# Sliding-window attention with a gated convolution on one Trainium2 core: the band mask of 18 of 32 score units moved from VectorE into TensorE's sum

## Chip, core and metric

The kernel runs on one core of one Trainium2 chip. The metric is the device time of one execution in microseconds, lower is better. Before the change it takes 223.1 us (median of three runs: 222.8, 223.1, 225.12).

The page names the engines PE (TensorE, matmuls), PEld (its weight loads), DVE (VectorE), ACT (ScalarE), POOL (GpSimd) and SP (SyncE, which here only issues DMAs).

## What is computed

Eight batches, eight heads, 576 positions, head size 64. Each position attends to the positions at most 32 away; the result feeds a feed-forward block with a three-tap convolution along the sequence as its gate.

```python
scores = scale * np.matmul(q, k.transpose(0, 1, 3, 2))
mask = np.abs(pos[:, None] - pos[None, :]) <= 32
scores = np.where(mask, scores, -1000000000.0)
attn = softmax(scores)                      # over the last axis
x = (attn @ v), heads side by side          # (8, 576, 512)
h = np.maximum(x @ w_in, 0.0)               # (8, 576, 1024)
conv_out[:, s] = sum over k of conv_w[k] * h[:, s + k - 1]
out = (h * sigmoid(conv_out)) @ w_out       # (8, 576, 512)
```

## The kernel before

**Order.** The whole kernel is one list of steps, the string `ORDER` (lines 29 to 96). Each word is a step with its arguments, and a number behind `@` is the PSUM bank it starts at. The steps are issued in this order, and a pinning helper at line 175 keeps every engine to it, so nearly all instructions carry line 175 in the profile and groups are told apart by their tiles. An engine that waits holds up all that stands behind it in its own queue.

**Attention.** A batch `b` has two groups `G` of four heads. `lq`, `lk`, `lv` load float32 q, k, v through SP's queue; `cq`, `ck`, `cv`, `vo` cast them to bf16 (last argument: `p` POOL, `a` ACT, `d` DVE; `vo` is v shifted by 64 rows); `tq`, `tk` transpose q and k on DVE (tiles `qT`, `kT`). Each group is cut into two halves `h` of four or five blocks of 64 queries, which gives 8 x 2 x 2 = 32 score units. For one unit:

- `sc` (line 240) makes the scores of 64 queries against 128 keys per block and head in four PSUM banks, one bank per head. Each head lies on 32 partitions with two bf16 halves (`e`) of its 64 dimensions, so a block takes 4 heads x 2 = 8 matmuls of 32 rows and 64 columns: 32 (h = 0) or 40 (h = 1) in a unit.
- `ex` takes the exponential on ACT into the tile `attn`, 1024 or 1280 columns.
- `mk` (line 266) multiplies `attn` by a 0/1 band on DVE, in place.
- `av` multiplies with v on PE; a column of ones in v makes the sums. `nr` takes the reciprocal of these and scales on DVE into the tile `xn`.

`xt` transposes `xn` into `xT` by DMA; the first two batches do it on PE (`xp`) with a copy (`xe`).

**Feed-forward.** The sequence is cut into chunks of 384 rows, three for two batches, 12 in all; the first two chunks are worked in halves, which gives 14 pieces `P`. For each piece and each quarter `m2` of the 1024 channels: `ph` (8 matmuls with `w_in`), `re` (ReLU on ACT), `pc` (convolution), `th` (tanh on ACT), `ga` (gate on DVE, into `gT`). The convolution has several forms: `P` six full matmuls; `A` and `D` twelve matmuls of 64 x 64, of which `A` then takes three ACT instructions in `th` and two DVE instructions in `ga`, and `D` one ACT and three DVE instructions; `X` no matmul, but two ACT instructions and four DVE instructions (`tp`). Each chunk ends with three `py` (8 matmuls of 512 columns with `w_out`), `ye` (copy out of PSUM) and `st` (store).

**Start.** `li`, `ci` load and cast `w_in`, `lo`, `co` `w_out`; `cw`, `dg` make diagonal matrices of the convolution weights; `s0` to `s7` fill constants.

Of the kernel before, what the change touches and what calls it, by code (L numbers as in the profile page):

```python
# [34 lines left out]
av,0,0,1@4 lv,1,0 ci,2,p ph,0,0@0 nr,0,0,1 ci,3,p ph,0,2@6 re,0,0 lo,2 pc,0,0,P@7 re,0,2 ci,1,p xp,0,3@4 th,0,0,P
xp,0,4@5 lo,3 xe,0,3,a ph,0,3@6 ga,0,0,P ck,1,0,p xe,0,4,a xp,0,2@4 re,0,3 ph,0,1@7 xe,0,2,a lo,1 cq,1,0,p tk,1,0
pc,0,3,P@5 re,0,1 ph,1,3@4 th,0,3,P tq,1,0 lk,2,1 cq,1,1,p pc,0,1,P@6 re,1,3 ph,2,0@7 th,0,1,P ga,0,3,P sc,1,0,0@0
re,2,0 lo,0 ck,1,1,p tq,1,1 ph,2,2@4 ex,1,0,0 ph,1,0@5 ga,0,1,P re,2,2 lv,1,3 cv,1,1,p sc,1,0,1@0 mk,1,0,0,d re,1,0
ph,2,3@4 ex,1,0,1 tk,1,1 lv,1,4 cv,1,2,p pc,0,2,P@5 ph,2,1@6 re,2,3 vo,1,1,d th,0,2,P lk,2,0 cv,1,0,p sc,1,1,0@0
re,2,1 ph,1,2@4 ga,0,2,P ex,1,1,0 mk,1,0,1,d pc,1,0,P@5 lq,2,0 co,2,p re,1,2 mk,1,1,0,d ph,1,1@6 th,1,0,P pc,1,2,P@4  # L40
vo,1,0,d re,1,1 lq,2,1 co,3,p sc,1,1,1@0 th,1,2,P ga,1,0,P pc,1,3,P@6 ex,1,1,1 ga,1,2,P pc,1,1,P@5 lk,3,0 co,1,p s6
pc,2,1,P@4 th,1,3,P mk,1,1,1,d av,1,1,0@0 th,1,1,P av,1,0,0@2 th,2,1,P lv,2,1 ck,2,1,p ga,1,1,P pc,2,0,P@7 nr,1,0,0
pc,2,3,P@5 th,2,0,P nr,1,1,0 pc,2,2,P@2 lq,3,0 co,0,p tk,2,1 xp,1,1@3 xp,1,0@0 xe,1,1,a py,0,0@1 lv,2,0 cv,1,3,p
xe,1,0,a ga,1,3,P ga,2,0,P th,2,2,P lk,4,0 vo,1,2,d cv,1,4,a py,0,2@0 ye,0,0,a vo,1,3,d th,2,3,P lv,2,2 ck,2,0,p
ga,2,1,P ph,3,2@1 ga,2,3,P ye,0,2,a ga,2,2,P ph,3,0@3 st,0,0 cq,2,0,p re,3,2 tk,2,0 av,1,1,1@4 re,3,0 av,1,0,1@6
nr,1,1,1 lk,3,1 cq,2,1,p py,1,0@0 nr,1,0,1 lq,3,1 ck,3,0,p ph,3,3@4 tq,2,1 ye,1,0,a xp,1,2@1 lv,2,3 cv,2,1,p re,3,3
pc,3,2,P@0 tq,2,0 xe,1,2,a sc,2,1,0@2 th,3,2,P ph,3,1@6 ex,2,1,0 st,1,0 ga,3,2,P cq,3,0,p xp,1,3@1 tk,3,0 pc,3,0,P@7
re,3,1 xe,1,3,a xp,1,4@4 lv,2,4 cv,2,0,p pc,3,3,P@5 th,3,0,P mk,2,1,0,d pc,3,1,P@6 xe,1,4,a vo,2,0,d sc,2,1,1@0 st,0,2
ck,4,0,p th,3,1,P py,0,1@4 ex,2,1,1 ga,3,1,P ga,3,0,P lq,4,0 tq,3,0 th,3,3,P cv,2,2,p lq,4,1 sc,2,0,0@0 ye,0,1,a
ph,4,0@6 vo,2,1,p ga,3,3,P ex,2,0,0 tk,4,0 st,0,1 sc,2,0,1@0 ck,3,1,p re,4,0 ph,4,2@4 mk,2,1,1,d ex,2,0,1 lv,3,1  # L50
mk,2,0,0,d cq,3,1,p pc,4,0,P@6 tk,3,1 re,4,2 lk,4,1 cv,2,3,p av,2,0,0@0 lv,3,0 th,4,0,P mk,2,0,1,d vo,2,2,p av,2,1,0@2
py,1,1@4 ga,4,0,P lk,5,1 cv,2,4,p tq,3,1 lv,3,2 ph,4,3@6 vo,2,3,p ye,1,1,a nr,2,0,0 lq,5,0 pc,4,2,A@4 nr,2,1,0 re,4,3
cq,4,0,p av,2,1,1@0 th,4,2,A lv,3,4 pc,4,3,A@2 nr,2,1,1 cq,4,1,p av,2,0,1@6 xt,2,0 th,4,3,A ga,4,2,A ph,4,1@0 cv,3,1,p
xt,2,1 nr,2,0,1 re,4,1 ga,4,3,A sc,3,0,0@4 ck,4,1,p xt,2,2 pc,4,1,P@0 ex,3,0,0 tq,4,0 cv,3,0,p sc,3,1,0@2 th,4,1,P
lv,3,3 mk,3,0,0,d py,1,2@6 vo,3,0,p ex,3,1,0 ga,4,1,P xt,2,3 mk,3,1,0,d py,2,1@7 ye,1,2,a cv,3,2,p xt,2,4 vo,3,1,d
cq,5,0,p sc,3,0,1@0 ye,2,1,a lk,5,0 av,3,1,0@4 tk,4,1 ex,3,0,1 py,2,2@6 st,1,1 cv,3,4,p nr,3,1,0 lv,4,0 ck,5,1,p
mk,3,0,1,d lv,4,1 av,3,0,0@4 sc,3,1,1@0 st,2,1 nr,3,0,0 py,2,0@7 ex,3,1,1 tq,5,0 xt,3,1 cv,3,3,p tq,4,1 vo,3,2,p
sc,4,0,0@0 ye,2,0,a ph,5,0@4 ex,4,0,0 xt,3,0 vo,3,3,d ph,5,2@0 ck,5,0,p re,5,0 st,1,2 mk,4,0,0,d ye,2,2,a lq,6,0
mk,3,1,1,d ph,5,3@2 lq,5,1 re,5,2 tk,5,0 st,2,2 cv,4,0,p av,3,0,1@0 re,5,3 av,3,1,1@4 nr,3,0,1 lv,4,2 cv,4,1,p
pc,5,2,D@6 st,2,0 vo,4,0,p pc,5,0,A@2 nr,3,1,1 th,5,2,D lv,4,4 ph,5,1@0 th,5,0,A lv,4,3 ga,5,2,D xt,3,3 ph,6,2@4  # L60
re,5,1 ga,5,0,A pc,5,1,X@6 pc,5,3,A@0 cq,6,0,p lk,6,0 re,6,2 tp,5,1,X ph,6,0@2 th,5,3,A xt,3,4 cq,5,1,p ph,6,1@4
re,6,0 ga,5,3,A xt,3,2 th,5,1,X pc,6,2,A@2 cv,4,2,p re,6,1 ga,5,1,X pc,6,0,A@0 th,6,2,A lq,6,1 pc,6,1,A@4 vo,4,1,d
lk,7,0 py,3,1@6 cv,4,4,p lq,7,0 th,6,0,A ga,6,2,A lv,5,1 cv,4,3,p th,6,1,A ga,6,0,A py,3,0@7 lq,7,1 vo,4,3,d ye,3,1,a
vo,4,2,d sc,4,1,1@0 lk,6,1 ck,6,0,p ye,3,0,a py,3,2@6 ex,4,1,1 st,3,1 ga,6,1,A lv,5,2 mk,4,1,1,d sc,4,0,1@0 ye,3,2,a
ph,7,1@4 lv,5,3 tk,5,1 ex,4,0,1 tq,5,1 ph,6,3@6 re,7,1 st,3,0 mk,4,0,1,d cq,6,1,p av,4,0,0@4 re,6,3 lv,5,0 sc,4,1,0@0
nr,4,0,0 ex,4,1,0 pc,6,3,A@6 tk,6,0 lv,5,4 cv,5,1,p ph,7,0@4 th,6,3,A mk,4,1,0,d ck,7,0,p lk,7,1 pc,7,1,A@0 ga,6,3,A
re,7,0 av,4,1,0@2 th,7,1,A pc,7,0,A@4 tq,6,0 st,3,2 ck,6,1,p py,4,0@6 th,7,0,A ga,7,1,A cq,7,0,p nr,4,1,0 av,4,1,1@0
ye,4,0,a cv,5,2,p ga,7,0,A xt,4,0 av,4,0,1@2 py,4,1@6 cv,5,3,p nr,4,1,1 xt,4,1 nr,4,0,1 ph,7,2@0 ye,4,1,a cv,5,0,p
vo,5,1,d xt,4,2 sc,5,1,0@2 re,7,2 cv,5,4,p py,4,2@6 vo,5,0,d ex,5,1,0 xt,4,3 vo,5,3,d sc,5,0,0@0 ye,4,2,a lv,6,1
ph,7,3@4 ex,5,0,0 lv,6,0 mk,5,1,0,d xt,4,4 vo,5,2,d av,5,1,0@6 re,7,3 pc,7,2,A@0 mk,5,0,0,d lv,6,4 ph,8,0@2 th,7,2,A  # L70
nr,5,1,0 lv,6,3 st,4,0 cv,6,1,p lv,6,2 av,5,0,0@4 ga,7,2,A re,8,0 pc,7,3,A@6 st,4,1 st,4,2 nr,5,0,0 pc,8,0,A@2
cv,6,0,p th,7,3,A ph,8,3@0 xt,5,0 vo,6,0,d th,8,0,A ga,7,3,A ph,8,1@4 cv,6,4,p lv,7,0 re,8,3 ga,8,0,A xt,5,1 py,5,0@6
cv,6,3,p re,8,1 vo,6,3,d pc,8,1,X@0 sc,5,1,1@2 lv,7,4 tp,8,1,X ye,5,0,a cv,6,2,p py,5,2@7 ex,5,1,1 st,5,0 vo,6,1,p
pc,8,3,A@2 mk,5,1,1,d th,8,1,X vo,6,2,p lv,7,1 ph,8,2@4 tq,7,0 ye,5,2,a th,8,3,A st,5,2 lv,7,3 ga,8,1,X ph,9,3@6
# [559 lines left out]
```

## Time and profile before

| | |
|---|---|
| median of three runs | 223.1 us |
| the profiled execution | 223.78 us |
| its span on the core | 221.8 us |
| TensorE's granted clock | 1.00 of full speed |
| PE busy | 192.9 us (87%) |
| DVE busy | 190.1 us (86%) |
| ACT busy | 162.3 us (73%) |
| POOL busy | 94.2 us (42%) |

The span counts from the first to the last recorded instruction; about 2 us of the execution lie outside it. Busy time of PE counts pipelined matmuls from start to modelled end, so it contains short gaps between matmuls. A group's mean is the time of one instruction from start to end; where instructions follow each other closely they start somewhat sooner than that.

### The profile page before, as it was taken

To read this page: it belongs to the slowest core of one execution; us is meant where nothing else is said; L and a number is where in the kernel's file an instruction comes from. 1 tells how busy PE (TensorE), PEld (TensorE's weight loads), DVE (VectorE), ACT (ScalarE), POOL (GpSimd) and SP (SyncE) were. 2 spreads that over 40 slices of the span, in tenths; PEclk is the share of its full clock that TensorE was granted. 3 is DMA by queue.
4 is the path that set the end of the run, shared out by engine and by line. 5 is a ranking of instruction groups with operands and counts; after the bars stand their busy time and mean duration, and the time that the engine had idled before them with its cause. 6 is when DMAs were issued, how large, how long until landed. Compare 5 with 4: busy or idle time off the path is not lost.

```text
span 221.8 us, 7235 instructions
## 1 busy us (share of the span) xinstructions
PE 192.9 (87%) x3026; PEld 114.5 (52%) x3026; DVE 190.1 (86%) x321; ACT 162.3 (73%) x260; POOL 94.2 (42%) x113
## 2 busy tenths in 40 slices
PE   1044999799999899899998999999999999999993
...
DVE  4989688999999989999999788996998777999820
...
DMA  6999989999999999999998999814204361121323
GB/s 214 333 263 386 339 254 351 354 318 350 284 313 300 137 133 258 250 260 193 369 332 178 222 230 244 222 53 106 98 3 145 69 136 50 38 79 42 142 101 136
DMA packets 65348, 45.96 MB, mean 207 GB/s; under 512 B 53516, under 2 KB 55588, under 8 KB 65316
## 3 DMA queue, kind: packets, MB, share of 16 engines
...
## 4 chain that ended last, share of the span: by engine, by line
PE 41%; DVE 40%; ACT 9%; issue 4%; POOL 3%; DMA 1%; ACTq 0%; DVEq 0%; POOLq 0%
PE PS L175 41%; DVE gT L175 9%; DVE attn L175 6%; DVE xn L175 6%; DVE kT L175 5%; DVE vo L175 5%; DVE qT L175 4%; ACT hT L175 3%; ACT z L175 3%; DVE diag_w L175 2%; ACT attn L175 2%; POOL qb L175 2%; DVE PS L175 2%; ACT PS L175 2%; DMA conv_w<-in_moe_conv_w_dram 1%
## 5 line engine op out<-in xcount | busy, mean ns | idle before, releaser
L175 PE MATMUL PS<-xT,w_in_sb 128*128 128x385 bf16 (+3 forms) x448 | 71.4, 309 | 1.2 <-DVE xn L175 0.5
L175 PE MATMUL PS<-w_out_sb,gT 128*128 128x512 bf16 x288 | 66.7, 380 | 0.1
L175 PEld LDWEIGHTS <-w_in_sb 128*128 128x128 bf16 x448 | 41.5, 100 | 25.7 <-issue 5.2
L175 POOL TENSOR_SCALAR qb<-st 128x1152 bf16<-128x1152 f32 x31 | 37.6, 1214 | 40.2 <-issue 8.9
L175 ACT ACTIVATE hT<-PS 128x770 bf16<-128x770 f32 (+3 forms) x56 | 40.2, 721 | 11.8 <-PE PS L175 10.8
L175 ACT ACTIVATE attn<-PS 128x1024 bf16<-128x1024 f32 (+1 forms) x32 | 36.0, 1132 | 11.2 <-PE PS L175 11.2
L175 DVE SCALAR_TENSOR_TENSOR gT<-PS,hT 128x384 bf16<-128x384 f32 (+2 forms) x66 | 40.2, 617 | 4.2 <-ACT PS L175 3.4
L175 PEld LDWEIGHTS <-gT 128*128 128x128 bf16 x288 | 26.5, 98 | 30.2 <-issue 0.9
L175 ACT ACTIVATE PS<-PS 128x384 f32<-128x384 f32 (+1 forms) x56 | 31.9, 572 | 6.2 <-PE PS L175 5.0
L175 POOL TENSOR_SCALAR ve<-vst 128x512 bf16<-128x512 f32 x38 | 28.4, 754 | 15.5 <-PE PS L175 11.6
L175 DVE TENSOR_TENSOR attn<-attn,mask 128x1024 bf16<-128x1024 bf16 (+1 forms) x32 | 29.3, 923 | 6.2 <-ACT attn L175 6.0
L175 ACT COPY y<-PS 128x512 f32<-128x512 f32 x36 | 20.8, 585 | 17.7 <-PE PS L175 17.7
L175 PE MATMUL PS<-hT,diag_w 64*64 64x384 bf16 (+2 forms) x456 | 31.1, 311 | 2.8 <-DVE gT L175 1.2
L175 DVE TENSOR_TENSOR xn<-PS,rec 128x512 bf16<-128x512 f32 (+1 forms) x32 | 26.4, 824 | 1.4 <-DVE rec L175 0.3
L175 PE MATMUL PS<-qT,kT 32*128 32x64 bf16 x1152 | 15.4, 195 | 11.7 <-DVE kT L175 9.3
L175 ACT ACTIVATE z<-PS 64x384 f32<-64x384 f32 x48 | 23.3, 485 | 0.9
L175 PEld LDWEIGHTS <-diag_w 64*64 64x64 bf16 (+1 forms) x456 | 18.3, 104 | 10.2 <-issue 6.3
L175 PEld LDWEIGHTS <-kT 32*128 32x128 bf16 x1152 | 11.9, 96 | 20.1 <-DVE kT L175 10.2
L175 DVE SCALAR_TENSOR_TENSOR PS<-hT,conv_w_sb,PS 128x384 f32<-128x384 bf16 x36 | 19.6, 618 | 1.6 <-ACT PS L175 1.6
L175 DVE STREAM_TRANSPOSE kT<-qb 128x576 uint32<-128x576 uint32 x16 | 19.7, 1240 | 0.7 <-PE PS L175 0.7
L175 PE MATMUL PS<-ve,attn 128*64 128x65 bf16 x384 | 16.4, 203 | 3.8 <-DVE attn L175 2.2
L175 DVE STREAM_TRANSPOSE qT<-qb 128x576 uint32<-128x576 uint32 x16 | 19.6, 1244 | 0.0
...
## 6 DMA issues: line engine op xcount, KB each, us to landing
...
```

The source lines that it names most:

```text
L175: return lambda *args, **kwargs: tc.keep_in_program_order(do(*args, **kwargs))
```

## The change

Three things change. First, `sc` gets an argument: in 18 of the 32 units (`m`) two constant matrices, `far` (a band of 0 and -1e9) and `unit` (an identity), are multiplied into the four banks before the scores are added on top: 8 matmuls more per unit, 32 rows each, 256 or 320 columns. These units have no `mk`. The other 14 units (`d`) are as before. Two new start-up steps make the matrices: `s9` on POOL for the first 32 partitions, `s10` copies them on ACT to the other three groups of 32. Second, the very last projection (chunk 11, rows 256 to 383) is made, copied and stored in two halves of 256 columns. Third, the whole of `ORDER` is new, and with it the place of many steps and the engine of some.

```diff
-    def sc(b, G, h, bank):
+    def sc(b, G, h, on, bank):
         where["sc", b, G, h] = bank
         qT, kT = qT_[unit(b, G) % NQT], kT_[unit(b, G) % NQT]
-        t0 = tiles_of(h)[0]
-        for t in tiles_of(h):
+        ts = tiles_of(h)
+        if on == "m":
             for e in range(2):
                 for a in range(4):
                     tensor.matmul(
-                        PS[:, bank + a, 64 * (t - t0):64 * (t - t0) + 64],
+                        PS[:, bank + a, 0:64 * len(ts)], far[32 * a:32 * a + 32, e, :],
+                        unit_[32 * a:32 * a + 32, e, None, :].broadcast_to([32, len(ts), 64]),
+                        start=(e == 0), stop=False,
+                    )
+        for i, t in enumerate(ts):
+            for e in range(2):
+                for a in range(4):
+                    tensor.matmul(
+                        PS[:, bank + a, 64 * i:64 * i + 64],
                         kT[32 * a:32 * a + 32, 64 * t:64 * t + 128, e],
                         qT[32 * a:32 * a + 32, 64 * t:64 * t + 64, e],
-                        start=(e == 0), stop=(e == 1),
+                        start=(e == 0 and on != "m"),
+                        stop=(e == 1 and (on != "m" or t == ts[-1])),
                     )
...
-    def py(c, i, bank):
-        where["py", c, i] = bank
+    def py(c, i, *x_bank):
+        *x, bank = x_bank
+        x = x[0] if x else None
+        where["py", c, i, x] = bank
+        n = d_model if x is None else 256
         for m in range(MB):
             tensor.matmul(
-                PS[:, bank, :], gT_[c % 3][:, m, 128 * i:128 * i + 128], w_out_sb[:, m, :],
+                PS[:, bank, 0:n], gT_[c % 3][:, m, 128 * i:128 * i + 128], w_out_sb[:, m, part(x)],
                 start=(m == 0), stop=(m == MB - 1),
             )
...
+    def s9():
+        gpsimd.memset(far[0:32], 0.0)
+        for base, sign in ((0, -1), (64, 1)):
+            gpsimd.affine_select(
+                out=far[0:32], in_=far[0:32], compare_op=ALU.is_ge, fill=-1e9, base=base,
+                pattern=[[32 * sign, 2], [-sign, 128]], channel_multiplier=sign,
+            )
+        gpsimd.memset(unit_[0:32], 0.0)
+        gpsimd.affine_select(
+            out=unit_[0:32], in_=unit_[0:32], compare_op=ALU.not_equal, fill=1.0, base=0,
+            pattern=[[-32, 2], [1, 64]], channel_multiplier=-1,
+        )
+
+    def s10():
+        for a in range(1, 4):
+            scalar.copy(out=far[32 * a:32 * a + 32], in_=far[0:32])
+            scalar.copy(out=unit_[32 * a:32 * a + 32], in_=unit_[0:32])
```

Of the new `ORDER`, the start and the end:

```diff
-lq,0,1 s3 s1 lq,0,0 s2 cw@0 lv,0,1 s5 s0 s7 lk,0,1 dg,4,d lk,0,0 lv,0,2 dg,2,d lv,0,3 dg,1,d cq,0,1,a lv,0,0 dg,7,d
-lv,0,4 dg,6,d dg,0,d li,0 cq,0,0,p tq,0,1 li,2 cv,0,1,p dg,5,d tq,0,0 li,3 ck,0,1,p s4 tk,0,1 li,1 ck,0,0,p dg,3,d
-sc,0,1,0@0 lk,1,0 cv,0,2,p sc,0,1,1@4 tk,0,0 ex,0,1,0 vo,0,1,p lq,1,0 ex,0,1,1 mk,0,1,0,d sc,0,0,0@0 lq,1,1 ex,0,0,0
+lv,0,2 s4 s1 s5 lq,0,0 s3 s2 lk,0,0 s0 lk,0,1 s7 lq,0,1 s9 lv,0,0 cw@0 lv,0,1 dg,4,d s10 li,2 dg,7,d li,0 dg,2,d
+dg,5,d lv,0,3 cq,0,0,a dg,6,d dg,3,d cv,0,2,a lv,0,4 ck,0,0,p tq,0,0 dg,0,d lq,1,1 ck,0,1,p tk,0,0 dg,1,d li,1
+cq,0,1,p sc,0,0,1,m@0 tk,0,1 sc,0,0,0,m@4 ex,0,0,1 li,3 cv,0,0,p tq,0,1 ex,0,0,0 lk,1,1 cv,0,1,p sc,0,1,0,m@0 vo,0,0,d
+sc,0,1,1,m@4 ex,0,1,0 lq,1,0 ci,2,p vo,0,1,d ex,0,1,1 lv,1,0 ci,0,p av,0,1,0@0 av,0,0,0@2 nr,0,1,0 lv,1,1 cv,0,3,a
+vo,0,2,p nr,0,0,0 lo,0 xp,0,1@0 xp,0,0@1 cv,0,4,p xe,0,1,a xe,0,0,a lk,1,0 cq,1,1,p vo,0,3,d ph,0,0@0 ph,0,2@1 re,0,0
...
-pc,13,1,A@6 ga,13,2,X ye,9,2,a pc,13,3,A@4 st,9,2 th,13,1,A py,10,0@0 th,13,3,A ga,13,1,A py,10,2@1 ye,10,0,a
-ga,13,3,A st,10,0 py,11,0@0 ye,10,2,a st,10,2 py,11,1@1 ye,11,0,a st,11,0 py,11,2@0 ye,11,1,a st,11,1 ye,11,2,a
-st,11,2
+re,13,2 tp,13,0,X py,10,0@0 re,13,3 th,13,1,X pc,13,3,A@2 ye,10,0,a ga,13,1,X th,13,0,X st,10,0 pc,13,2,D@0 py,10,2@4
+ga,13,0,X th,13,2,D ga,13,2,D th,13,3,A py,10,1@5 ye,10,2,a ga,13,3,A st,10,2 py,11,0@4 ye,10,1,a st,10,1 py,11,1@5
+ye,11,0,a st,11,0 py,11,2,0@4 ye,11,1,d py,11,2,1@6 st,11,1 ye,11,2,0,a st,11,2,0 ye,11,2,1,a st,11,2,1
```

Counted over the whole list, the steps whose number changes:

| step | before | after |
|---|---|---|
| `mk`, h = 0 / h = 1 | 16 / 16 | 6 / 8 |
| `sc` with the band, h = 0 / h = 1 | 0 / 0 | 10 / 8 |
| `cv` on POOL / ACT / DVE | 38 / 2 / 0 | 30 / 9 / 1 |
| convolution of a full piece: `P` / `A` / `D` / `X` | 2 / 24 / 5 / 9 | 0 / 18 / 15 / 7 |
| convolution of a half piece: `P` / `X` | 16 / 0 | 15 / 1 |
| `xe` on ACT / DVE | 10 / 0 | 9 / 1 |
| `ye` on ACT / DVE | 36 / 0 | 35 (two of 256 columns) / 2 |

The units with the band by batch 0 to 7: 4, 3, 4, 1, 4, 1, 1, 0.

More of the change, by code (lines that the diff above doesn't have):

```diff
@@ L35 @@
[L35 to L74, printed above, removed]
@@ new lines @@
+lo,2 ci,1,p pc,0,0,P@0 re,0,2 tq,1,1 av,0,0,1@2 th,0,0,P lv,1,4 av,0,1,1@4 ci,3,p ga,0,0,P ph,0,1@1 nr,0,0,1
+pc,0,2,P@0 re,0,1 lo,1 ck,1,1,p ph,0,3@6 nr,0,1,1 th,0,2,P pc,0,1,P@7 re,0,3 ga,0,2,P lo,3 cq,1,0,p xp,0,3@4 th,0,1,P
+pc,0,3,P@5 tk,1,1 xe,0,3,a xp,0,2@6 th,0,3,P xp,0,4@0 lv,1,3 cv,1,0,p xe,0,2,a tq,1,0 xe,0,4,a ph,1,1@4 lv,1,2
+cv,1,1,p ga,0,3,P ph,2,0@6 re,1,1 ga,0,1,P vo,1,0,p ph,1,0@5 re,2,0 lk,3,0 pc,2,0,X@4 pc,1,1,P@7 re,1,0 sc,1,1,0,d@0
+tp,2,0,X co,0,p th,1,1,P ph,1,3@6 ex,1,1,0 lv,2,0 pc,1,0,P@5 ga,1,1,P ck,1,0,p re,1,3 ph,2,2@0 mk,1,1,0,d th,2,0,X
@@ new lines @@
+lk,2,0 co,2,p th,1,0,P pc,1,3,P@6 re,2,2 ph,2,1@7 tk,1,0 lq,2,0 ph,2,3@0 re,2,1 cv,1,4,p ga,2,0,X ph,1,2@7 re,2,3
+ga,1,0,P lk,2,1 co,1,p sc,1,0,0,m@0 re,1,2 th,1,3,P pc,2,3,P@4 ex,1,0,0 ga,1,3,P pc,1,2,P@5 lq,3,0 co,3,p th,2,3,P
+sc,1,0,1,m@0 th,1,2,P s6 ga,2,3,P lq,2,1 cv,1,3,p py,0,0@6 ex,1,0,1 ga,1,2,P vo,1,3,d cv,1,2,a lv,2,4 py,0,1@7
+vo,1,2,d vo,1,1,d lv,2,3 av,1,0,1@4 ye,0,0,d ye,0,1,a lv,2,2 cv,2,0,p av,1,1,0@0 nr,1,0,1 av,1,0,0@2 py,0,2@6 st,0,0
+ck,2,0,p nr,1,1,0 nr,1,0,0 pc,2,1,P@7 lv,2,1 cq,2,0,p ye,0,2,a tk,2,0 xp,1,1@4 th,2,1,P xp,1,0@5 xe,1,1,a sc,1,1,1,m@0
@@ new lines @@
+pc,6,3,A@0 ck,6,1,p re,7,0 av,4,0,1@4 cv,5,1,a av,4,1,0@2 cq,6,1,p nr,4,0,1 th,6,3,A ph,7,1@6 nr,4,1,0 vo,5,0,p
+ph,7,3@4 re,7,1 ga,6,3,A xt,4,1 cv,5,2,p sc,4,1,1,m@0 re,7,3 vo,5,1,p xt,4,0 pc,7,0,A@6 tk,6,0 ex,4,1,1 py,4,1@4
+cv,5,3,p th,7,0,A lv,6,1 tq,6,0 lv,6,0 vo,5,2,p av,4,1,1@0 ga,7,0,A ye,4,1,a pc,7,3,A@2 st,4,1 ck,7,0,p nr,4,1,1
+pc,7,1,D@4 lv,6,2 th,7,3,A py,4,0@6 cq,7,0,p xt,4,4 th,7,1,D ga,7,3,A cv,5,4,p ga,7,1,D sc,5,1,0,m@0 ye,4,0,a xt,4,2
+cv,6,1,p ph,7,2@6 ex,5,1,0 vo,5,3,d xt,4,3 cv,6,0,p sc,5,0,0,d@0 re,7,2 py,4,2@4 vo,6,0,d ex,5,0,0 lv,6,3 lv,6,4
@@ new lines @@
+th,8,2,A ga,8,1,D py,5,0@2 th,8,3,D ga,8,2,A ph,9,0@4 ye,5,0,a ga,8,3,D st,5,0 av,5,1,1@0 re,9,0 pc,9,3,D@2 nr,5,1,1
+cv,7,2,p cv,7,0,a pc,9,0,A@4 cv,7,4,a cv,7,3,p pc,9,1,A@6 cv,7,1,d xt,5,2 th,9,0,A vo,7,3,p py,6,1@0 th,9,1,A ga,9,0,A
+xt,5,4 py,6,2@1 ye,6,1,a vo,7,1,p ga,9,1,A th,9,3,D xt,5,3 ga,9,3,D sc,6,0,1,d@4 vo,7,0,p ye,6,2,a py,6,0@0 st,6,1
+ex,6,0,1 st,6,2 vo,7,2,p mk,6,0,1,d sc,6,0,0,d@2 ye,6,0,a ph,10,3@6 ex,6,0,0 st,6,0 tk,7,1 sc,6,1,1,d@0 re,10,3
+ph,10,1@4 mk,6,0,0,d ex,6,1,1 tq,7,1 av,6,0,1@6 re,10,1 sc,6,1,0,m@0 nr,6,0,1 pc,9,2,A@4 ex,6,1,0 mk,6,1,1,d
@@ new lines @@
+av,6,0,0@6 th,9,2,A av,6,1,0@0 nr,6,0,0 ph,10,0@2 nr,6,1,0 av,6,1,1@6 ga,9,2,A xt,6,1 re,10,0 pc,10,1,A@0 nr,6,1,1
+pc,10,0,D@2 th,10,1,A xt,6,0 pc,10,3,D@4 py,7,1@6 th,10,0,D ga,10,1,A xt,6,2 ga,10,0,D ph,10,2@0 ye,7,1,a xt,6,3
+th,10,3,D py,7,0@2 re,10,2 ga,10,3,D st,7,1 pc,10,2,X@6 xt,6,4 py,7,2@3 ye,7,0,a tp,10,2,X st,7,0 ph,11,0@4 ye,7,2,a
+st,7,2 th,10,2,X ph,11,1@0 re,11,0 ga,10,2,X sc,7,1,0,d@2 re,11,1 py,8,1@6 ex,7,1,0 mk,7,1,0,d sc,7,0,0,d@0 ye,8,1,a
+pc,11,0,D@4 ex,7,0,0 st,8,1 py,8,0@6 th,11,0,D mk,7,0,0,d ga,11,0,D av,7,0,0@0 ye,8,0,a ph,11,2@2 st,8,0 nr,7,0,0
@@ L154 @@
     mask = tiles(1, [128, 4 * 5 * 64], BF16, "mask")[0]
+    far = tiles(1, [128, 2, 128], BF16, "far")[0]
+    unit_ = tiles(1, [128, 2, 64], BF16, "unit")[0]
     mask1 = tiles(1, [128, 64], BF16, "mask1_")[0]
@@ L492, with part, ye, sto @@
     out_rows = out.rearrange("b s f -> (b s) f")
-    def py(c, i, bank):
-        where["py", c, i] = bank
+    def part(x):
+        return slice(0, d_model) if x is None else slice(256 * x, 256 * x + 256)
+    def py(c, i, *x_bank):
[3 more added lines that the diff above has]
+        n = d_model if x is None else 256
         for m in range(MB):
             tensor.matmul(
-                PS[:, bank, :], gT_[c % 3][:, m, 128 * i:128 * i + 128], w_out_sb[:, m, :],
+                PS[:, bank, 0:n], gT_[c % 3][:, m, 128 * i:128 * i + 128], w_out_sb[:, m, part(x)],
                 start=(m == 0), stop=(m == MB - 1),
             )
-    def ye(c, i, e):
-        copy(e, y_[(3 * c + i) % NY], PS[:, where["py", c, i], :])
-    def sto(c, i, e="s"):
+    def ye(c, i, *x_e):
+        *x, e = x_e
+        x = x[0] if x else None
+        n = d_model if x is None else 256
+        copy(e, y_[(3 * c + i) % NY][:, part(x)], PS[:, where["py", c, i, x], 0:n])
+    def sto(c, i, x=None):
         r0 = c * CH + 128 * i
-        {"s": sync, "a": scalar}[e].dma_start(out_rows[r0:r0 + 128, :], y_[(3 * c + i) % NY])
+        sync.dma_start(out_rows[r0:r0 + 128, part(x)], y_[(3 * c + i) % NY][:, part(x)])
     def li(p, e="s"):
```

53 lines of the change are left out of this document (32 added, 21 removed).

## The prediction

> **What bounds the kernel now.** I read the page first. Two engines are nearly full and share the chain that ended last; the slices show DVE full in the first two thirds, PE at the end, and the DMA engines full for the first 26 slices (143 us).
>
> ```profile
> PE 192.9 (87%) x3026; PEld 114.5 (52%) x3026; DVE 190.1 (86%) x321; ACT 162.3 (73%) x260; POOL 94.2 (42%) x113
> ...
> PE   1044999799999899899998999999999999999993
> ...
> DVE  4989688999999989999999788996998777999820
> ...
> DMA  6999989999999999999998999814204361121323
> ...
> PE 41%; DVE 40%; ACT 9%; issue 4%; POOL 3%; DMA 1%; ACTq 0%; DVEq 0%; POOLq 0%
> ```
>
> Next the windows of 10 us (start:end, length, busy and count of PE, PEld, DVE, ACT, POOL, clock, DMA share, GB/s):
>
> ```profile
> 60.00:70.00 10.00, 9.04 (x151) 5.09 (x154) 9.92 (x14) 5.76 (x9) 9.32 (x11) 1.00 1.03 303
> 70.00:80.00 10.00, 8.78 (x165) 4.66 (x155) 9.83 (x17) 7.46 (x12) 8.66 (x10) 1.00 1.36 181
> 160.00:170.00 10.00, 10.00 (x144) 5.18 (x142) 9.81 (x20) 9.39 (x16) 0.00 (x0) 1.00 0.18 49
> 200.00:210.00 10.00, 9.96 (x70) 4.81 (x69) 9.25 (x15) 9.49 (x17) 0.00 (x0) 1.00 0.18 71
> ```
>
> From 40 to 120 us DVE is at 91 to 99% and PE has holes; after 120 PE is full. The chain in order of time agrees: mostly DVE pieces up to 119 us, then long PE pieces such as these (start, length, what):
>
> ```profile
> 119.14 8.72 PE PS L175 x145
> ...
> 152.02 18.22 PE PS L175 x288
> ...
> 200.29 17.82 PE PS L175 x104
> 218.13 0.58 ACT y L175
> ```
>
> Last, prices, from the groups with shapes kept apart (busy time, mean ns) and from the timeline (start, length):
>
> ```profile
> L175 DVE TENSOR_TENSOR attn<-attn,mask 128x1280 bf16<-128x1280 bf16 x16 | 15.4, 964 | 2.1 <-ACT attn L175 2.1
> L175 DVE TENSOR_TENSOR attn<-attn,mask 128x1024 bf16<-128x1024 bf16 x16 | 14.1, 881 | 4.0 <-ACT attn L175 3.9
> ```
>
> ```profile
> 85.57 0.42 PE L175 MATMUL PS<-qT,kT 32*128 32x64 bf16 x32
> 85.92 4.09 PE L175 MATMUL PS<-xT,w_in_sb 128*128 128x385 bf16 x24
> ...
> 208.18 1.17 PE L175 MATMUL PS<-hT,diag_w 64*64 64x384 bf16 x24
> 209.29 8.81 PE L175 MATMUL PS<-w_out_sb,gT 128*128 128x512 bf16 x40
> ```
>
> A unit of 32 score matmuls holds the queue from 85.57 to 85.92, 0.35 us, 11 ns each. Forty matmuls of 512 columns take 8.81 us, some 0.17 of it the drain of the last: 216 ns each, 0.42 ns a column. Twenty-four convolution matmuls of 384 columns take 1.11 us to the next start, 46 ns each, where one alone streams 384 x 0.42 = 161: nearly four run at once.
>
> **The masks.** Removed on DVE: 10 x 0.881 + 8 x 0.964 = 16.5 us. Added on PE: 8 matmuls a unit. No row shows 32 rows with 256 columns. From below: four at once, as the convolution, give two rounds of 256 x 0.42 = 0.21 us, 0.27 for 320 columns. From above: one after the other, 8 x 256 x 0.42 = 0.86, and 1.08. The score matmuls are the nearest row: same 32-row groups, same four banks, and they start every 11 ns although 64 columns stream in 27, so at least 2.4 run at once. I take 0.23 and 0.28: 10 x 0.23 + 8 x 0.28 = 4.5 us (ends 4.3 and 17.2; no gain is possible, since the score matmuls stay). The Trainium skill (TensorE: Matmul & The Clock Gate, Part 3, measured speedup) has four row tiles 3.07 times as fast as one, not 4 times; by that figure the sum would be an estimated 5.6 us, and no row here shows it.
>
> `av` no longer stands behind `mk`. The new matmuls wait only for their banks. `s9` and `s10` cost nothing: POOL idles from 3.9 to 6.55 us in the old run, and behind `s10` on ACT stands the first cast of q, whose result DVE cannot take before its six `diag_w` products end at 8.3. Without that cover six small copies cost about 1.5 us.
>
> **The rest, queue by queue.** A full-piece convolution costs PE 0.58 as `A` or `D`, 0.98 as `P`, 0 as `X`; DVE 1.14 as `A` (two gates back to back), 1.57 as `D` (three), 0.95 as `P`, 3.15 as `X` (four `tp` at 0.55, one gate); ACT 1.45, 0.80, 0.80, 1.90.
>
> - PE: 4 more `A`/`D` +2.3, two `P` fewer -2.0, one half `P` fewer -0.5, masks +4.5; unrounded +4.4.
> - DVE: masks -16.5, `A` -6.8, `D` +15.7, `P` -1.9, `X` -6.3, half `X` +1.3, the four copies moved to it +2.2: -12.3.
> - ACT: `cv` +4.4, tanh -3.9, `X` -1.5, `xe` and `ye` -1.6, `s10` +1.5: -1.1.
> - POOL: eight `cv` at 0.754 fewer, `s9` +1.3: -4.7.
> - SP and DMA: the same loads, transposes and stores, one store cut in two.
>
> PE's work at these rates (36 `py` at 1.73, 40 full `ph` at 1.35, 16 half ones at 0.665, `sc` 0.355 or 0.415, `av` 0.42 or 0.63, the convolutions) is 184.8 us before and 189.2 after. DVE falls from 190 to 178.
>
> **The start.** The old first scores begin at 13.16 us, the first `ph` at 24.49. The new list loads 256 KB of v and then q and k of one group (1.4 MB; before, 2.0 MB until that pair was there), so DVE is the limit: six `diag_w` until 8.3, `tq` 1.17, `diag_w` 0.64, `tk` 1.17, scores at 11.3. The four masks (0.82, 1.48 and 1.54 of them on the chain) are gone, and two of the four `av` now stand behind `ph`. Late next is ACT: four exponentials in a row end near 16.5; then `av`, two `nr` at 0.85, `xp`, two `xe`. The two pieces of `w_in` that are needed have 4.1 MB up to them, which the old run had moved by 15.6 us. First `ph`: 20.0 (19 to 24.5).
>
> **The middle and the end.** Before, from the first `ph` to 121.4 us PE did 86.9 us of work in 96.9: 10.0 idle, beside 90.0 of DVE work. From there to 218.1 it did 93.2 in 96.7: 3.5 idle, beside 81.4 of DVE. At a ratio of DVE to PE work of 1.04 idle was 10.3%, at 0.87 it was 3.6%. The same two stretches after (cut in piece 7) have ratios 77.5 / 83.9 = 0.92 and 85.7 / 100.8 = 0.85; I take 5.5% and 3.6% of PE's time: 4.6 + 3.6 us. PE would end at 20.0 + 184.7 + 8.2 = 212.9. Behind it lay 3.7 us; the copy of half width saves 0.2. Span 216.4, execution 2.0 more, 218.4 beside 223.78; the median of the runs lay 0.7 below, so 217.7.
>
> What is late next are the loads. The last of the five casts of batch 6's v waited for its load in the old run:
>
> ```profile
> 134.63 0.68 POOL L175 TENSOR_SCALAR ve<-vst 128x512 bf16<-128x512 f32 x1 [0.44 <-DMA vst<-in_v_dram]
> ```
>
> PE had 104.2 us of work ahead of that step then, and has 104.4 after, with the same transfers in SP's queue before it. By PE's sum it comes at 125.1 now. In windows of half a microsecond the DMA share up to 135 us falls short of 1 by some 13 us in all (without the first 2), mostly during the transposes and while SP waits for DVE or ACT. If half of that goes, the load is there at 128. The cast is now on ACT, which would hold `re` behind it; PE has two `py` (3.5 us) to run first. So 125.1 + 3.5 against 128 plus the cast and a `re` (0.6 + 0.8): about 1 us late, and as much at the earlier casts moved to ACT taken together, I put 1.5 in all. Forecast 217.7 + 1.5 = 219.2.
>
> **The rivals.**
> - The loads bind (slower). If the DMA engines lose no hole, the load lands at 134.6 as before, and from there PE has 84.8 us to do where it had 80.6: 4.2 more, less 0.2 in the tail, 227.1. It turns to a loss when the load lands later than 130.6. For it: the DMA line, and 19 us of POOL's waits are for q, k and v. Against it: DVE at 98% over the same stretch, and SP stood 39 of the first 130 us waiting for engines. 12%.
> - The masks do not overlap (slower). One after the other PE gets 17.2 instead of 4.5: 219.2 + 12.7 = 231.9; the gain is lost at 4.5 + 3.9 = 8.4 us, 0.47 a unit. Against it the score row. 8%.
> - No change. Half of the start's gain goes (+2.2), or idle stays as it was (+5.3), or the loads take 3 us more: 221 to 224.5. For it: ACT, at 93 to 97% in the late windows, now holds nine casts that wait for loads. 22%.
> - No load is late and idle is 3.6% throughout, start at 19: 217.7 - 1.6 - 1.0 = 215.1, down to 212.5 if idle halves once more. 13%.
> - That a mask stays or is lost: the list shows 14 `mk` and 18 `m`, nothing for it.
>
> **Numbers.** Forecast 45%, own range 216 to 221. The range of 8 in 10 leaves out the masks' rival, half of the loads' and the bottom of the low one: 212.5 to 226.5. What lies within 1% (220.9 to 225.3) can hardly be told from no change: 22%. Slower 20% (loads and masks). Faster 58%.
>
> **What would show it.** The eight matmuls of `far` and `unit` hold PE for 0.21 to 0.28 us; DVE busy near 178, PE near 197, ACT near 161; first `ph` near 20; windows from 40 to 120 us with PE above 9.5. I am wrong if DVE is still at 98% there, if the first `ph` comes after 23, or if ACT's waits for loads add up to more than 5 us.

## The result and the profile after

The changed kernel takes 229.8 us (median of four runs, 228.4 to 230.8) beside 222.95 us for the kernel before on the same chip (222.4 to 225.1): a ratio of 1.028, 95% interval 1.021 to 1.036. It is slower; the forecast was 219.2 us, faster. The profiled execution took 229.47 us, its span is 227.7 us. Here and below a median is of all runs of a kernel, while ratios and intervals leave out runs more than 1.5% above its fastest, so that the two can differ by a per cent (e14: 230.3 us beside 1.023).

Busy engines, two of the slices and the chain on the page of the changed kernel:

```profile
PE 198.2 (87%) x3185; PEld 120.1 (53%) x3208; DVE 176.9 (78%) x317; ACT 161.9 (71%) x257; POOL 86.8 (38%) x110
...
PE   1386989999999689998979879999999999999994
...
DVE  7786667699789997688669677998898477798851
...
DMA  6999999999999999995999979412314325123123
...
PE 37%; DMA 19%; DVE 19%; ACT 10%; SPq 5%; issue 5%; POOL 2%; ACTq 0%; DVEq 0%
```

DVE lost 13 us, and PE has five more. The stretch from 40 to 120 us in one window, before and changed (columns as in the prediction):

```profile
40.00:120.00 80.00, 73.52 (x1226) 43.75 (x1225) 77.74 (x121) 59.06 (x97) 48.44 (x53) 1.00 1.07 273
40.00:120.00 80.00, 72.35 (x1339) 43.95 (x1348) 66.52 (x114) 56.83 (x90) 41.47 (x48) 1.00 1.05 281
```

DVE went from 97% to 83% there, and PE did not fill up: 9.0 us of 10, where the forecast had more than 9.5. The DMA engines are as full as before and as long, some 140 us, and the chain now runs over transfers for 19% of the span, where it had 1%. The windows that the prediction showed, of the changed kernel (same columns):

```profile
60.00:70.00 10.00, 9.30 (x193) 5.33 (x194) 7.73 (x14) 5.92 (x9) 4.69 (x5) 1.00 1.05 378
70.00:80.00 10.00, 8.00 (x208) 4.69 (x206) 9.62 (x17) 8.82 (x13) 6.79 (x9) 1.00 1.16 245
160.00:170.00 10.00, 9.80 (x256) 6.21 (x257) 8.80 (x16) 8.08 (x12) 0.48 (x1) 1.00 0.22 82
200.00:210.00 10.00, 9.95 (x53) 5.13 (x53) 9.00 (x17) 8.76 (x15) 0.00 (x0) 1.00 0.36 110
```

In the last two PE is nearly as full as before (9.8 and 9.95 us). Most of what was lost lies earlier; behind the start the emptiest stretch is this, first in windows of 20 us, then in the chain in order of time (start, length, what), both of the changed kernel:

```profile
95.00:115.00 20.00, 18.43 (x304) 10.27 (x299) 15.21 (x27) 14.49 (x22) 6.93 (x9) 1.00 0.93 250
115.00:135.00 20.00, 15.61 (x272) 8.54 (x274) 15.09 (x28) 14.09 (x23) 12.47 (x16) 1.00 1.04 218
```

```profile
123.68 2.15 DVE gT L176 x3
...
126.99 1.22 SPq L176
128.21 0.05 issue
128.26 4.20 DMA xT<-xn
132.46 0.79 issue
133.25 1.48 PE PS L176 x8
```

Between 115 and 135 us PE is busy for 15.6 of 20 us, DVE for 15.1 and ACT for 14.1: no engine is full, but the DMA share is 1.04. The `ph` at 133.25 had waited for a transpose of `xn` that took 4.2 us among the loads. (From issue to landing a transpose takes 3.7 us in the median of e3, below, and 2.5 us in e9, the same kernel without most loads.) The waits on the DMA engines' work, of the changed kernel (total, times, longest; before, the same three were 8.6, 6.8 and 3.5 us):

```profile
POOL qb L176 <- DMA st<-in_q_dram: 21.5, 10, 11.5
POOL qb L176 <- DMA st<-in_k_dram: 14.5, 9, 3.5
POOL ve L176 <- DMA vst<-in_v_dram: 14.4, 9, 6.0
```

The masks cost on TensorE what was forecast. One unit in the timeline of the changed kernel:

```profile
50.77 0.66 PE L176 MATMUL PS<-xT,w_in_sb 128*128 128x193 bf16 x6
51.37 0.40 PE L176 MATMUL PS<-unit,far 32*128 32x256 bf16 x8
51.60 0.41 PE L176 MATMUL PS<-qT,kT 32*128 32x64 bf16 x32
```

The eight matmuls hold the queue from 51.37 to 51.60, 0.23 us. In the records of the units that wait for nothing it is 228 to 230 ns for 256 columns and 281 for 320, and four start within some 10 ns: four at once. The second and the fourth unit of batch 0, at half clock (last section), take 0.41 and 0.52 us.

### The profile page after: what moved, and what is told of

The parts are those of the page before. It is cut to its first block, busy times and chain, and to the rows that moved or that the text cites. A ratio compares the mean times of both kernels' runs of the same rounds, so it can differ in the third digit from the quotient of the medians.

```text
span 227.7 us, 7568 instructions
## 1 busy us (share of the span) xinstructions
PE 198.2 (87%) x3185; PEld 120.1 (53%) x3208; DVE 176.9 (78%) x317; ACT 161.9 (71%) x257; POOL 86.8 (38%) x110
## 4 chain that ended last, share of the span: by engine, by line
PE 37%; DMA 19%; DVE 19%; ACT 10%; SPq 5%; issue 5%; POOL 2%; ACTq 0%; DVEq 0%
PE PS L176 37%; DMA vst<-in_v_dram 7%; DVE gT L176 7%; SPq L176 5%; DVE xn L176 4%; DMA out_dram<-y 4%; DMA st<-in_q_dram 4%; ACT hT L176 4%; DMA xT<-xn 4%; ACT PS L176 3%; DVE PS L176 2%; DVE qT L176 2%; DVE vo L176 1%; DVE rec L176 1%; DVE attn L176 1%
## 5 line engine op out<-in xcount | busy, mean ns | idle before, releaser
L176 PE MATMUL PS<-w_out_sb,gT 128*128 128x512 bf16 (+1 forms) x273 | 64.5, 373 | 2.5 <-DVE xn L176 0.6
L176 DVE SCALAR_TENSOR_TENSOR gT<-PS,hT 128x384 bf16<-128x384 f32 (+2 forms) x86 | 49.9, 585 | 12.7 <-ACT PS L176 11.7
L176 POOL TENSOR_SCALAR qb<-st 128x1152 bf16<-128x1152 f32 x31 | 37.4, 1215 | 43.5 <-DMA st<-in_q_dram 21.5
L176 ACT ACTIVATE attn<-PS 128x1280 bf16<-128x1280 f32 (+1 forms) x32 | 36.1, 1130 | 5.8 <-PE PS L176 5.5
L176 ACT COPY y<-PS 128x512 f32<-128x512 f32 (+1 forms) x35 | 20.1, 573 | 18.9 <-PE PS L176 17.1
L176 PE MATMUL PS<-hT,diag_w 64*64 64x384 bf16 (+1 forms) x486 | 30.5, 314 | 1.3 <-ACT hT L176 1.0
L176 POOL TENSOR_SCALAR ve<-vst 128x512 bf16<-128x512 f32 x30 | 19.5, 660 | 22.6 <-DMA vst<-in_v_dram 14.4
L176 DVE SCALAR_TENSOR_TENSOR PS<-hT,conv_w_sb,PS 128x384 f32<-128x384 bf16 (+1 forms) x32 | 16.9, 591 | 3.2 <-ACT PS L176 3.0
L176 PE MATMUL PS<-qT,kT 32*128 32x64 bf16 x1152 | 15.6, 195 | 3.9 <-DVE kT L176 3.3
L176 DVE COPY vo<-ve 64x520 bf16<-64x520 bf16 x38 | 14.4, 380 | 5.8 <-POOL ve L176 4.4
L176 PEld LDWEIGHTS <-attn 128*64 128x64 bf16 x640 | 13.3, 117 | 9.6 <-issue 4.6
L176 POOL TENSOR_SCALAR vo<-vst 64x512 bf16<-64x512 f32 x26 | 17.3, 667 | 1.9
```

The source lines that it names most:

```text
L176: return lambda *args, **kwargs: tc.keep_in_program_order(do(*args, **kwargs))
```

## The experiments

Each ratio is against the kernel before on the same chip. "The old order with masks" is the old list with the same 18 units added by TensorE.

**The four corners: order, masks, loads.** e1 and e2 leave out loads (59 of the 72 loads of q, k and v, not 68 as the first expectation says; the casts read what lies there), e3 makes the mask part alone, e4 the order alone.

```diff
 e1, e2: lists without lq and lk from batch 2 on and without lv from batch 1 on
-lq,2,0 ... lk,2,0 ... lv,1,0 ... lv,7,4
 e3: the old list
-sc,0,1,0@0 ... ex,0,1,0 ... mk,0,1,0,d
+sc,0,1,0,m@0 ... ex,0,1,0
 e4: the new list
-sc,0,0,1,m@0 tk,0,1 sc,0,0,0,m@4 ex,0,0,1
+sc,0,0,1,d@0 tk,0,1 sc,0,0,0,d@4 ex,0,0,1 mk,0,0,1,d
```

> The changed kernel without the loads of q and k from batch 2 on and of v from batch 1 on (68 of 72 us-scale loads of the later batches left out, their casts read what the buffers still hold, so the output is that of old data). Theory L (the loads set the pace up to about 137 us, and the new order has as much TensorE work ahead of each load as the old one): PE's idle time falls to what the sum had, 8 us behind the first ph, and the time to 218 us (214 to 221). Theory O (the new order holds itself up in the engines' in-order queues, whatever the loads do): 226 us or more, PE still with holes of 1 us and more behind ACT and DVE.

> The old order, masks on VectorE, with the same loads left out. If VectorE bound the first 120 us of the old kernel, as the prediction had it, the loads cost it little: 219 to 222.5 us, DVE still at 97% from 40 to 120 us. If the loads bound it as well: below 216 us.

> The old order with only the mask part of the change: the same 18 units get their band from TensorE and have no mask step, with the two start-up steps for the constants. No other step is moved. Theory L: the loads of batches 5 to 7 still land when they did, and PE has 4.5 us more to do, 2 of them behind 134 us: 222 to 226 us. If VectorE was the only bound: 16 us less on it before 175 us, and with the idle shares of the prediction 214 to 219 us. Theory O says the masks were never the harm: not above 223 us.

> The new order with all 32 masks back on VectorE, each right behind its exponential; the constants and the 18 x 8 matmuls are gone. Theory L: VectorE has slack in the new order (177 of 228 us), PE gets 4.5 us back: 225 to 230 us. If the masks on TensorE help the new order by VectorE's 16 us: 236 us and more. If they harm it: 224 us or less.

Together with e9, the same loads left out of the old order with masks:

> Old order with the mask part, without the loads of q and k from batch 2 on and of v from batch 1 on (the casts read what lies there). Theory L: the stretch up to 135 us is held twice, by VectorE's work and by the stream of loads, so that taking one away alone gave nothing (223.5 without the mask on VectorE, 225.8 without the loads); both away together give 212 to 219. Theory W: TensorE is held by the order's own waits between engines, and the loads only end at the same time: 222 to 225.

| | loads as they are | loads left out |
|---|---|---|
| old order, masks on DVE | 1 | 1.011 (1.006 to 1.016), e2 |
| old order, masks on PE | 0.995 (0.990 to 0.999), e3, 223.5 us | 0.986 (0.981 to 0.991), e9, 220.1 us |
| new order, masks on DVE | 1.067 (1.061 to 1.072), e4 | |
| new order, masks on PE | 1.028 (1.021 to 1.036), the change | 1.004 (1.000 to 1.007), e1, 224.8 us |

Three things follow. Masks on TensorE never hurt: they are worth 0.5% in the old order, 2.5% there without the loads, nearly 4% in the new one. The new order, with the forms and engines of its list, does the harm: 3.4% with the masks on PE, 1.8% of it without the loads too. And taking the loads away wins nothing as long as the masks hold DVE, 0.9% once they are gone, 2.4% in the new order. e3 and e4 came as one of their theories had it. e1 fell between its two (214 to 221, 226 or more), so each holds a part. e2 was slower than either of its own: without the loads the old kernel takes 1.1% longer, for a reason that is not shown (three of its four runs have a step of half clock, see the last section, and a mean of 0.992), and the 2.5% contains this. All runs of e4 have two such steps (0.984 to 0.986), so the 4% is in part theirs. e9 also missed what both theories gave (212 to 219, 222 to 225): the loads are a second bound behind VectorE, but one worth some 3 us, not ten.

Where it happens is seen in windows of 20 us from 55 to 135 us. The kernel before:

```profile
55.00:75.00 20.00, 17.81 (x355) 10.94 (x352) 19.79 (x28) 14.88 (x25) 18.07 (x21) 1.00 1.17 280
75.00:95.00 20.00, 19.20 (x353) 10.74 (x345) 18.93 (x27) 13.38 (x18) 12.43 (x14) 1.00 1.07 205
95.00:115.00 20.00, 18.95 (x285) 10.06 (x284) 19.46 (x33) 18.58 (x32) 7.72 (x8) 1.00 1.01 292
115.00:135.00 20.00, 18.81 (x263) 9.97 (x263) 17.04 (x36) 14.78 (x26) 8.55 (x12) 1.00 1.02 223
```

The old order with masks (e3):

```profile
55.00:75.00 20.00, 19.41 (x385) 11.14 (x383) 17.05 (x25) 15.34 (x23) 15.85 (x21) 1.00 1.08 286
75.00:95.00 20.00, 19.94 (x318) 11.03 (x316) 17.15 (x29) 14.27 (x22) 9.58 (x12) 1.00 1.11 215
95.00:115.00 20.00, 17.74 (x298) 9.61 (x296) 14.33 (x25) 17.21 (x29) 7.65 (x8) 1.00 1.01 286
115.00:135.00 20.00, 17.49 (x254) 9.26 (x252) 14.21 (x32) 13.36 (x23) 7.42 (x10) 1.00 1.01 199
```

The same without loads (e9):

```profile
95.00:115.00 20.00, 18.77 (x305) 10.25 (x303) 15.45 (x28) 18.28 (x32) 4.72 (x5) 1.00 0.14 48
115.00:135.00 20.00, 19.35 (x302) 10.31 (x301) 17.95 (x35) 15.02 (x26) 9.11 (x14) 1.00 0.39 85
```

With the masks gone PE fills up from 55 to 95 us (37.0 to 39.4 of 40) and empties from 95 to 135 (37.8 to 35.2): it has run ahead into a stretch that the DMA engines pace. Take their loads away and it is at 38.1 there. The same can be put as a backlog: the time at which a step starts on PE, less PE's work ahead of it in the list at the prediction's rates. It grows only where PE idles or runs slowly. An entry can move by about a microsecond if the cut falls a step later.

| last `ph` or `sc` with PE work ahead of it | before | old order with masks (e3) | changed kernel | e3 without loads (e9) |
|---|---|---|---|---|
| up to 24 (37 to 41 us) | 22.7 | 18.9 | 21.5 | 20.3 |
| up to 80 (102 to 109 us) | 29.4 | 22.3 | 25.8 | 24.0 |
| up to 112 (136 to 145 us) | 31.8 | 27.1 | 33.2 | 25.6 |
| the last `ph` | 33.0 | 28.7 | 33.9 | 26.9 |
| work in all | 184.8 | 189.3 | 189.2 | 189.3 |

At the second row the kernel before is behind e3 by 7.1 us and behind the changed kernel by 3.6. Up to the third e3 gives back 2.4 of it and the changed kernel 5.0, and each pays 4.5 for the mask matmuls. Net, with the last row: e3 equal (33.0 - 28.7 - 4.5 = -0.2), the changed kernel 5.3 us behind; the spans differ by 0.3 and 5.9. Behind the third row the columns differ by less than a microsecond.

**Which stretch of the new order.** Four lists follow one order to a cut and then take the steps that are left from the other, all with the masks on TensorE.

```diff
 e5, at 26 us: new, then old
 th,0,0,P lv,1,4 av,0,1,1@4 ci,3,p ga,0,0,P
+lv,1,2 nr,0,1,1 nr,0,0,1 xp,0,3@4 xp,0,4@5
 e8, at 72 us: new, then old
 pc,4,0,A@4 nr,2,1,1 vo,3,0,p
+th,4,0,A ga,4,0,A lk,5,1 ph,4,3@6
 e6, at 134 us: new, then old
 lv,7,1 nr,5,1,0 cv,6,3,p
+ga,7,2,D re,8,0 pc,8,0,A@2 ph,8,3@0
 e7, at 130 us: old, then new
 pc,8,0,A@2 cv,6,0,p th,7,3,A
+ga,7,3,A vo,6,0,d cv,6,2,a lv,7,0
```

> New order up to the second unit of the first convolution piece (about 26 us), then the steps that are left in the old order; the masks on TensorE as in the change. It tells the new start alone. Nothing after 30 us is new. If the cost of the new order lies behind the start (middle or end), this run is at or below the old order with the mask part (223.5): 220 to 223, with the earlier first convolution (20.75 instead of 22.7 us) kept for 0 to 2 us. If the start itself does the harm (loads of q, k and v in another order on SP's queue), it is at 226 to 230.

> New order up to the third projection unit of piece 4 (72 us), then the steps that are left in the old order. Theory A (between 72 and 134 us): 221 to 224. If the cost is already made by 72 us (the loads of batches 3 to 5 are issued later from the start of the middle): 227 to 230. Theory B (end): 221 to 224.

> New order up to the second projection unit of piece 8 (134 us), then the steps that are left in the old order. Theory A, the cost lies between 72 and 134 us, where casts and transposes wait for loads of q, k and v that start later: 228 to 230, as the change. Theory B, the cost lies in the end, where the new order has more convolution work for ScalarE and VectorE beside the last projection: 222 to 225. Theory C, it is spread: 226 to 227.

> Old order with the mask part up to the second projection unit of piece 8 (130 us), then the steps that are left in the new order, with the last projection in column halves. Theory A (middle): 222 to 224. Theory B (end): 227 to 230. Theory C: 225 to 226.

Measured: e5 228.4 us (1.021, 1.015 to 1.027), e8 226.2 (1.009, 1.005 to 1.012), e6 230.5 (1.030, 1.023 to 1.037), e7 228.2 (1.017, 1.010 to 1.023). By their expectations e5 would put the harm into the start and e7 into the end. But a joint has a price of its own: right behind its cut e5 has a hole of PE of 2.55 us, e7 one of 3.99, which neither whole list has. At the first row of the table above e5 stands at some 26, where the changed kernel, with the same start, has 21.5; at the third e7 stands at some 30, where e3, the same up to 130 us, has 27.1. So e5 and e7 say little. e8 and e6 share their start and their end, and their steps differ in place and form between 72 and 134 us only: e6 takes 2.1% longer, 4.3 us between the medians. Both have a joint, and that of e8 is not free (PE is busy for 1.44 of the 3.4 us behind 73.7 us, last section). From the second row to the third the backlog grows by 1.7 us in e8 and by 8.4 in e6, of which some belongs to e6's joint at 134 us; the changed kernel has no joint and grows by 7.4 there, between 102 and 145 us.

**What in that stretch: transposes, casts, masks.** e10, e11 and e18 take DMA transposes away and make them by matmul as the first two batches do (15, those of batches 2 to 4; in e18 the five of batch 4). e12 puts nine casts of v back on POOL. e17 adds the last three masks of batch 3 on TensorE, where the windows from 70 to 85 us showed DVE at 97%.

```diff
 e10 (old order), e11 (new), e18 (old, batch 4 only)
-ph,4,1@0 cv,3,1,p xt,2,1 nr,2,0,1 re,4,1
+ph,4,1@0 cv,3,1,p xp,2,1@5 nr,2,0,1 re,4,1 xe,2,1,a
 e12 (new)
-cv,0,3,a ... cv,1,2,a ... cv,6,4,a ... cv,7,1,d
+cv,0,3,p ... cv,1,2,p ... cv,6,4,p ... cv,7,1,p
 e17 (new)
-sc,3,1,0,d@0 xt,2,3 ex,3,1,0 ... mk,3,1,0,d
+sc,3,1,0,m@0 xt,2,3 ex,3,1,0
```

> Old order with the mask part; the 15 DMA transposes of xn for batches 2, 3 and 4 are made as those of batches 0 and 1 are: four matmuls with the identity and a copy out of PSUM, on VectorE and ScalarE in turn. Theory L: the DMA engines lose about 15 x 1.2 us of work (estimate from the share of busy DMA) before 135 us, TensorE gains 3.2 us, and the loads of batch 6 land at 117 to 125 instead of 135: 216 to 221. Theory W: only the work is added: 225 to 229.

> The change with the same 15 transposes taken from the DMA engines. Theory L: its order lost about 5 us to the loads (229.8 against 224.8 without them), and these come back less 3 us of TensorE: 224 to 228. Theory W: 231 to 235.

> Old order with the mask part and the five transposes of batch 4 made by TensorE instead of the DMA engines (1.0 us more for TensorE, about 6 us less for the DMA engines, as an estimate from the share of busy DMA). If the late loads of batches 5 and 6 are worth what the run without loads showed (3.4 us for all of them): batch 6's v lands at 130 to 132 instead of 135.5, and the time is 221.5 to 223 (ratio 0.987 to 0.994 of the kernel before). If the order absorbs it: 224 to 225 (0.998 to 1.003).

> The change with its eight casts of v that ScalarE and VectorE took over put back to GpSimd, in the same places of the order. If the change loses because a cast that waits for a late load holds ScalarE's queue (exp, relu and tanh behind it): 225 to 228. If that is no cause: 229 to 233, as GpSimd has 6 us more to do.

> The change with batch 3's other three masked units added by TensorE too (all four of batch 3). If VectorE's 98% in 70 to 85 us makes the holes of TensorE there, VectorE loses 2.8 us, TensorE gains 0.8 us of work and the holes of 75 to 79 us shrink by 1 to 2 us; the loads of v that wait for the casts come no sooner, so the time falls by 0.5 to 1.5 us: 228.3 to 229.3 (ratio 1.023 to 1.027). If these holes are waits of the order itself, or the late loads absorb it: 229.5 to 230.5 (1.028 to 1.033).

Measured: e10 227.2 us (1.014, 1.009 to 1.019), e11 230.0 (1.029, 1.024 to 1.034), e18 223.3 (0.999, 0.994 to 1.003), e12 231.0 (1.033, 1.024 to 1.042), e17 230.2 (1.026, 1.019 to 1.033).

Taking the transposes away did what it was to do to the DMA engines: the last load of batch 6's v is there at some 126.5 us in e10 (its cast, which waited for it, starts at 126.54) and at 127.9 in e18 (135.4 in e3), and at about 130 in e11 (136.3 in the changed kernel). In e11 the backlog between the second and the third row of the table grows by 3.3 us instead of 7.4. But some 1 us is lost ahead of the second row and the matmuls cost 3.1 us of PE, so nothing is left over, and in the old order nothing was won at all: e10 is slower than e3, e18 no faster, with batch 6's v 7 to 9 us earlier. So the transfers make part of the changed kernel's hole between 95 and 135 us, and this way of relieving them costs as much as it brings. The casts are no cause: e12 is no faster than the change. e17's interval covers both of its expectations, so its time decides nothing. In its trace DVE fell from 4.80 to 3.86 us in the window from 75 to 80 us, and PE did not rise (3.80 to 3.33); from 70 to 85 us DVE fell from 14.6 to 12.8 and PE rose by 0.6 (12.4 to 13.0), less than the 0.8 us of the added matmuls. That speaks against VectorE as the reason for those holes, but it is one trace.

**The start.** e16 loads the last two chunks of batch 0's v ahead of the weights. e13 and e14 keep PE busy with matmuls that nobody reads, since the first `ph` ran at half rate (below). e15 leaves the masks of batches 3 to 7 on VectorE.

```diff
 e13 (old order with masks), e14 (new, 16 for 20)
-cw@0 ... xp,0,1@0
+wu,2@7 cw@0 wu,20@7 ... wu,4@7 xp,0,1@0
+def wu(n, bank):
+    for i in range(n):
+        tensor.matmul(
+            PS[:, bank, :].rearrange("p (a x) -> p a x", a=4), ident,
+            ident[:, None, :].broadcast_to([128, 4, 128]), start=True, stop=True,
+        )
 e16 (new)
-lv,0,1 dg,4,d s10 li,2 dg,7,d li,0 dg,2,d dg,5,d lv,0,3
+lv,0,1 lv,0,3 lv,0,4 dg,4,d s10 li,2 dg,7,d li,0 dg,2,d dg,5,d
 e15 (old): m for the 11 units of batches 0 to 2
-sc,3,0,0,m@0 ... ex,3,0,0
+sc,3,0,0,d@0 ... ex,3,0,0 ... mk,3,0,0,d
```

> Old order with the mask part, and matmuls on the identity whose result nobody reads, put where TensorE waits anyway: 22 from the identity's end to the first scores (2.2 to 13 us) and 4 before the first transposes by matmul (18.7 to 20.2 us). Theory C: TensorE's half clock up to 23 to 27 us is paid by everything done before it; kept busy, it gets the full clock by 10 to 14 us, the first projection units take 83 ns a matmul instead of 155, and the time falls by 1.5 to 3 us: 220.5 to 222. Without Theory C (the early stage waits for loads, VectorE and ScalarE): 223 to 225.

> The change with the same idle matmuls (18 before the first scores, 4 before the first transposes). Theory C: the early start of the first piece was lost because it ran at half clock; 226 to 228. Without it: 229 to 231.

> Old order, the masks of batches 0, 1 and 2 alone on TensorE (11 of the 18 units), the seven others on VectorE again. Theory P: behind 65 us a unit's eight matmuls cost TensorE 0.25 us and VectorE's time is worth nothing there: 7 x 0.25 = 1.8 us less than with all 18 (0.9946 of the kernel before): 0.985 to 0.99 of it, 220.5 to 222. Against it: VectorE's seven masks, 6.4 us, come back in full where loads and VectorE hold the middle together: 223.5 to 226.

> The change with the loads of the last two chunks of batch 0's v put in front of the first weight loads on SP's queue. If its start waits for them (the second half of batch 0's attention is normalised at 25.8 to 27.9 us, against 22.4 to 24.5 in the old order): 227 to 229. If the place of that step in TensorE's order decides, no change: 229 to 231.

Measured: e13 223.4 us (1.000, 0.997 to 1.002), e14 230.3 (1.023, 1.016 to 1.031), e15 223.6 (0.999, 0.995 to 1.003), e16 230.8 (1.036, 1.032 to 1.040). Neither the clock nor the loads of batch 0 explain the lost lead: e16 is no faster than the change, and e14 is 0.5% faster, within the noise. e13 had the full clock for its first `ph` (83 to 84 ns a matmul) and started it at 22.7 us, as e3 did; between 15.2 and 22.0 us its clock was at half again, so it did not test a start at full clock throughout. Theory P of e15 fell as well: seven masks fewer on PE, 1.8 us, bought nothing.

The fastest kernel of the study is e3, the mask part in the old order: 0.995 of the time before, interval 0.990 to 0.999.

**What stays open.** Of the 3.4% between the new order and e3, about 1.5% goes with the loads (3.4 less the 1.8 that stay without them). The other 1.8%, some 4 us (e1 against e9), is spread over waits of 0.2 to 1.2 us between engines that each keep their order, and in half of e1's runs over a step or two of half clock; taking away one suspect at a time (casts, masks at 75 us, first loads, clock of the start) moved none of it beyond the noise. Which steps stand in the wrong place was not found, nor whether it is their place or their form that costs (the new list has 15 `D` for 5, and 18 `A` for 24, in full pieces): no run changes the forms alone.

## Why the prediction was wrong

- **The masks** were right: 18 of them gone from VectorE, 0.23 and 0.28 us a unit on PE at full clock, up to 0.52 in batch 0 at half clock, which the sum did not have. The rival of masks that do not overlap falls. By the figure that the prediction took from the Trainium skill (TensorE: Matmul & The Clock Gate, Part 3, measured speedup) it would have been 5.6; the trace disagrees: at 0.42 ns a column eight matmuls one after the other take 0.86 and 1.08 us, so four at once are 3.7 and 3.8 times as fast at these 256 and 320 columns, not 3.07 times, which the page has for 512.
- **The work by queue** was right: DVE 176.9 us (forecast 178), PE 198.2 (near 197), ACT 161.9 (161), POOL 86.8 (89.5).
- **The start** was right as a time, the first `ph` at 20.75 us (20.0, 19 to 24.5), and wrong in worth. Of a lead of 3.7 us over the kernel before, 1.2 was left at 40 us (first row of the table). The old start with the masks on TensorE led by 3.8 there.
- **The middle and the end** is the step that failed: idle time was taken to follow the ratio of DVE's to PE's work. Forecast 4.6 + 3.6 us; measured, as time less the forecast's work, 10.0 (20.75 to 114.6 us) and 9.1 (114.6 to 224.5), some 5 of the latter before 137 us. DVE was busy 83% from 40 to 120 us instead of 97%, and PE was no fuller. e3 shows that the rule was false and not merely its numbers: DVE at 173 us instead of 190 in the old order, and PE's backlog grew from the first row of the table to the last by 9.8 us, as before the change (10.3). What the runs show in its place is the new order with its forms and engines: 3.4% with the masks on TensorE in both lists, about half of it together with the loads; which of its steps hold PE up stays open. The no-change rival had this for the middle ("idle stays as it was", +5.3).
- **The loads** were late by more than was put. The last load of batch 6's v was to land at 128 us, because half of the DMA engines' holes would go; it landed at 136.3, after 134.6 before. The last cast came at 137.3 instead of 125.1 to 128. Between the second and third row of the table the changed kernel loses 5.0 us to the kernel before, where 1.5 was put for the loads; how much of it is theirs is not shown. The rival "the loads bind" (227.1 us, 12%) had this mechanism; its turning point of 130.6 us was passed by 5.7. (The rival of masks that do not overlap, 231.9 us, lies nearer to the measured time, by luck: the trace rules its mechanism out.) The loads were given too little because DVE at 98% was read as the reason why little else could bind. Both bound in the same stretch, and e2 against e9 shows it: without loads alone nothing is won, without both 1.4%. But the loads are not the whole: without them the changed kernel still takes 224.8 us (e1), where the forecast without its term for loads was 217.7.
- The sum: first `ph` +0.75, middle +5.4, end +5.5, the loads' own term -1.5 (it is in the idle time now), what lies behind PE's end -0.5: 9.6 us, from the forecast of 219.9 us for a profiled execution to 229.47.
- "Wrong if": two of the three signs did not come (DVE fell from 97% to 83%, the first `ph` was in time), the third did: ACT waited 5.3 us for loads. e12 shows that this sign pointed at the wrong thing: with those casts on POOL the time is no shorter.
